# First loads, diagonals by two engines and the place of a table load in an attention and feed-forward kernel

## The chip, the cores and the metric

The kernel runs on one core of one Trainium2 chip. The metric is the device time of one execution in microseconds (us). Five engines work side by side: PE (matmuls; PEld is its weight loading), DVE (VectorE), ACT (ScalarE), POOL (GpSimd) and SP, which only issues DMAs here. Each engine runs its own instructions in a fixed order, so an instruction that waits holds up all that stand behind it on the same engine.

## The reference

Three parts follow each other. All is computed in float32.

1. A linear attention with a decaying state, 4 batches, 8 heads, 768 tokens, 48 elements per head:

```
cur   = (u * k_t) outer v_t
y_t   = r_t @ (state + cur)
state = w * state + k_t outer v_t
```

2. On the 3072 x 384 result a feed-forward layer with 2048 hidden units: `h = x @ w_in; g = h * tanh(softplus(h)); x = g @ w_out`.
3. A second one with other weights: `h = x @ w_in; g = h if h > 0 else exp(h) - 1; out = g @ w_out`.

## The kernel before, in words

The tokens are cut into 24 chunks of 128 (six to a batch), four chunks to a block of 512 columns. The attention of block 0 comes first, with the conversion of the first weights beside it; then the first layer runs block by block with the attention of the next block woven in; then the second layer.

**A chunk of attention.** Two loads bring it: KR (r and k with the head's elements on partitions, 448 KB) and KVR (k, v and r with tokens on partitions, 576 KB). The third chunk borrows the tiles HB1 and TB for its KR and KVR. DVE multiplies k and r of KR by powers of the decay (Tn, T) at line 405, and k of KVR by Trv. Then:

- *scores* (L541, 8 matmuls, traced as 16): k against r, 128 x 128 per head, into two PSUM banks.
- *diagonal* (L509, 4 matmuls): the sums of u*k*r for each token. DVE first makes the product k*r in the tile XO (L405); PE sums it over the partitions against um; ACT copies the 128 x 8 result to CD. XO is one tile, so the next chunk's product waits until PE has read it.
- *AB*: ACT (L531) puts CD on the diagonal of a 128 x 8 x 128 tile, one ACTIVATE per head, for chunks 0 to 3 (`ON_ACT = 4`); from chunk 4 on POOL does it in one AFFINE_SELECT (L533). DVE (L548, two COPY_PREDICATED) then puts the scores above the diagonal.
- *outputs* (L611, L615, L620): state against r, and v against AB, into bank 6 alone. ACT casts the result to XH, DVE takes the rest to XL (L639); bank 6 is free only then. The first chunk of a batch has no L611.
- *update* (L580): the new part of the state in bank 5; DVE adds it to the decayed state SS (L595), which ACT (L590) has decayed.

**Other names.** w_in and w_out are split into a high and a low part (wih, wil, woh, wol): a raw tile (HB0 for the first, RAW0 and RAW1 after it) is loaded, DVE makes the high bits (L714, L717, L719), ACT casts them (L420), DVE subtracts (L412). The first layer's first matmul is L755 (nine per tile of 512 columns), its second L807; ACT takes its result to HB, applies three functions in TB with table loads between (L780 to L783), and casts to GH; DVE subtracts to GL. The second layer is L755 again with L1007 to L1009.

**What sets the order.** All work is first recorded as operations with the tiles they read and write and a cost in us. A planner (`Graph.order`) then walks through time, and on each engine takes the ready operation of lowest rank. Its result is the fixed order of every engine. Its costs are assumptions; when an instruction really starts is decided on the chip by the semaphores. So a change in a cost or in what an operation reads and writes can move instructions anywhere behind it. Each use of a PSUM bank for scores or first-layer tiles takes the next one in a cycle (`next_bank`).

`tables` (L822 on) makes T, Tn and Trv; its function `turn` turns T on PE (L854) through bank 7, and ACT copies that to Trv. The list of first loads stands in L883 to L897: w, chunk 0, um (by ACT's queue), u, chunk 1, the first raw weights, chunk 2, two more raw weights.

## Time and profile before

| | |
|---|---|
| median of 3 runs | 941.93 us (940.3, 941.93, 955.51) |
| profiled execution | 945.41 us, its span 943.6 us |
| PE busy | 916.8 us (97%) |
| PEld, DVE, ACT, POOL busy | 777.2, 597.9, 505.7, 173.5 us |
| chain of waits | PE 85%, DVE 6%, ACT 4%, DMA 4% |
| DMA | 90.83 MB |

The span runs from the first to the last instruction of the profiled execution. Busy shares are means over stages with different limits; PE's 97% says that most of the span is bound by matmuls, and not what bounds the first 100 us.

### The profile page before, as it was taken

What the parts mean: (1) busy time and instruction counts of PE and PEld (TensorE: products, weight loads), DVE (VectorE), ACT (ScalarE), POOL (GpSimd) and SP (SyncE); (2) the same over time, 40 slices, a digit from 0 to 9 for tenths busy, and PEclk for the clock granted to TensorE, in tenths of its full rate; (3) what the DMA queues carried; (4) which work ended last, traced back from release to release, by engine and by line L of the source; (5) the groups of instructions that cost most, each with busy time, mean ns of one, the idle gap of its engine ahead of it and who ended that gap; (6) DMA issues with size and microseconds to landing.
All of it is one profiled execution on the core that took longest, in us unless ns stands there. A gap on an engine that the chain in (4) does not pass through costs nothing.

```text
span 943.6 us, 13890 instructions
## 1 busy us (share of the span) xinstructions
PE 916.8 (97%) x5770; PEld 777.2 (82%) x5770; DVE 597.9 (63%) x777; ACT 505.7 (54%) x650; POOL 173.5 (18%) x125
## 2 busy tenths in 40 slices
PE   7888999999999999999999999999999999999997
PEld 6766777888878888888888899888899889889896
DVE  6799996443644454344376898678766555654663
ACT  4596678776777876787799643321411312312211
POOL 0011044333522264330222423000000000000000
PEclk9997999999999999999999999999899999999999
DMA  8355442220211311121233434878600101000001
GB/s 275 136 173 168 162 146 68 73 93 26 78 45 46 105 64 45 57 68 46 59 130 101 131 130 163 285 259 276 229 1 22 47 1 34 34 1 34 1 0 38
DMA packets 33335, 90.83 MB, mean 96 GB/s; under 512 B 3312, under 2 KB 6512, under 8 KB 33264
## 3 DMA queue, kind: packets, MB, share of 16 engines
q1 hardware_dynamic: 32848, 89.86, 28.6%
q8 instruction: 47, 0.77, 0.3%
q14 instruction: 24, 0.20, 0.1%
q10 hardware_dynamic: 416, 0.00, 0.0%
HBM read 80.42 MB, written 9.44 MB: 95 GB/s over the span
## 4 chain that ended last, share of the span: by engine, by line
PE 85%; DVE 6%; ACT 4%; DMA 4%; issue 1%; SPq 0%; DVEq 0%; ACTq 0%
PE bank L755 39%; PE bank L807 19%; PE bank L1009 6%; PE bank L1008 6%; PE bank L1007 6%; PE bank L541 3%; PE bank L611 1%; DMA RAW<-w2i 1%; DVE KVR L735 1%; PE bank L615 1%; PE bank L620 1%; PE bank L580 1%; DVE GL L412 1%; PE bank L509 1%; DMA RAW<-w1o 1%
## 5 line engine op out<-in xcount | busy, mean ns | idle before, releaser
L755 PE MATMUL bank<-XH,wih 128*128 128x512 f32 x576 | 230.8, 401 | 5.5 <-ACT HB L420 4.7
L755 PE MATMUL bank<-XL,wih 128*128 128x512 f32 x576 | 228.3, 396 | 1.6 <-DVE XL L639 1.6
L755 PE MATMUL bank<-XH,wil 128*128 128x512 f32 x576 | 228.7, 397 | 0.0
L992 ACT ACTIVATE HB<-HB 128x512 f32<-128x512 f32 x96 | 60.6, 633 | 236.3 <-DVE HB L990 235.6
L412 DVE TENSOR_TENSOR GL<-HB,GH 128x512 fp32r<-128x512 f32 (+2 forms) x75 | 91.2, 1216 | 84.8 <-PE bank L807 83.4
L755 PEld LDWEIGHTS bank<-XH,wih 128*128 128x128 f32 x576 | 109.0, 189 | 29.8 <-ACT HB L420 5.6
L1007 PE MATMUL bank<-woh,GH 128*128 128x384 f32 x384 | 131.0, 341 | 2.0 <-DVE GH L422 1.7
L755 PEld LDWEIGHTS bank<-XH,wil 128*128 128x128 f32 x576 | 108.8, 189 | 26.8 <-DVE wil L412 0.3
L1008 PE MATMUL bank<-wol,GH 128*128 128x384 f32 x384 | 130.9, 341 | 0.0
L755 PEld LDWEIGHTS bank<-XL,wih 128*128 128x128 f32 x576 | 108.9, 189 | 24.5 <-DVE XL L639 1.9
L420 ACT CAST GH<-HB 128x512 fp32r<-128x512 f32 (+2 forms) x74 | 71.8, 970 | 67.8 <-DVE HB L993 38.1
L990 DVE TENSOR_SCALAR HB<-bank 128x512 f32<-128x512 f32 x96 | 65.9, 688 | 56.9 <-PE bank L755 56.7
L993 DVE SCALAR_TENSOR_TENSOR HB<-HB,bank 128x512 f32<-128x512 f32 x96 | 65.6, 684 | 38.1 <-ACT HB L992 37.6
L405 DVE TENSOR_TENSOR HB<-HB,TB 128x1536 f32<-128x1536 f32 (+1 forms) x36 | 62.9, 1746 | 42.0 <-ACT TB L783 42.0
L807 PE MATMUL bank<-GH,woh 128*128 128x512 f32 x288 | 85.9, 399 | 0.0
L420 ACT COPY HB<-bank 128x512 f32<-128x512 f32 x89 | 51.6, 585 | 62.0 <-PE bank L755 53.0
L807 PE MATMUL bank<-GH,wol 128*128 128x512 f32 x288 | 84.7, 395 | 0.0
L807 PE MATMUL bank<-GL,woh 128*128 128x512 f32 x288 | 84.6, 395 | 0.0
L1007 PEld LDWEIGHTS bank<-woh,GH 128*128 128x128 f32 x384 | 72.8, 190 | 6.2 <-DVE GH L422 2.0
L1008 PEld LDWEIGHTS bank<-wol,GH 128*128 128x128 f32 x384 | 72.9, 190 | 3.2
L1009 PE MATMUL bank<-woh,XL 128*128 128x384 f32 x216 | 73.5, 340 | 0.1
L807 PEld LDWEIGHTS bank<-GL,woh 128*128 128x128 f32 x288 | 54.1, 188 | 13.2
(126 smaller groups left out, 1298.0 us busy)
## 6 DMA issues: line engine op xcount, KB each, us to landing
KVR<-kvr SPq DMA_DIRECT2D x23, 576.0 KB, 5.0
RAW<-w1o SPq DMA_DIRECT2D x16, 768.0 KB, 4.4
RAW<-w2i SPq DMA_DIRECT2D x16, 768.0 KB, 4.3
RAW<-w2o SPq DMA_DIRECT2D x16, 768.0 KB, 4.3
RAW<-w1i SPq DMA_DIRECT2D x15, 768.0 KB, 4.3
KR<-rk SPq DMA_DIRECT2D x23, 448.0 KB, 4.1
x2d<-XO SPq DMA_DIRECT2D x18, 256.0 KB, 2.0
AB<-x2d SPq DMA_DIRECT2D x18, 256.0 KB, 2.9
```

Of the source, the lines that this page charges most:

```text
L405: ENG[e].tensor_tensor(out=o, in0=a, in1=b, op=ALU.mult)
L412: ENG[e].tensor_tensor(out=o, in0=a, in1=b, op=ALU.subtract)
L420: A.copy(out=o, in_=a)
L541: mm(bks[i][:, p * CH:(p + 1) * CH], X[half[i], g, 1, j], X[half[i], g, 0, j], start=True, stop=True)
L755: mm(hbk[:, :n], w[f][:, k, :], x[:, k, :n], start=(i == 0), stop=(i == len(seq) - 1))
L807: mm(acc[:, :n], w[f0 + j][:, d * P:(d + 1) * P], gg[:, j, :n], start=(q == 0 and i == 0), stop=(q == NG - 1 and i == len(seq) - 1))
L990: on(DVE, dve(n), [kb], [kg], lambda: V.tensor_scalar(out=g, in0=hbk[:, :n], scalar1=0.0, scalar2=None, op0=ALU.min))
L992: on(ACT, act(n), [kg], [kg], lambda: A.activation(out=g, in_=g, func=AF.Exp), AF.Exp)
L993: on(DVE, dve(n), [kg, kb], [kg], lambda: V.scalar_tensor_tensor(out=g, in0=g, scalar=-1.0, in1=hbk[:, :n], op0=ALU.add, op1=ALU.max))
L1007: mm(acc, gh[:, tt], woh[f], start=(f == 0), stop=False)
L1008: mm(acc, gh[:, tt], wol[f], start=False, stop=False)
L1009: mm(acc, gl[:, tt], woh[f], start=False, stop=(f == NF - 1))
```

## The change

- The load of KVR leaves r out for chunks 0 to 7 (`FROM_PE = 8`), which use the diagonal on PE and never read it: 384 KB in place of 576 KB, in two pieces of 1536 bytes per partition in place of one of 4608.
- u_sb (192 KB), first read in chunk 8, is loaded after the raw weights and not before chunk 1.
- For chunks 0 to 3 the diagonal sums go to the next bank of the cycle and not to bank 5, which they shared with the state's update.
- For the same chunks ACT puts four of the eight heads on the diagonal, and POOL the other four. The planner is told 1.23 and 0.7 us where it had 2.45, and 1.25 in place of 1.4 for POOL's later ones.
- `turn` uses bank 6 and not bank 7.
- A copy of one column by ACT into a CD tile stands ahead of its other work, so that its table load does too.

```diff
--- before.py
+++ after.py
@@ -461,7 +461,8 @@
         s["X"], s["t"] = X, t
         gr_keys.update(key(a, i) for a in (X, t) for i in range(3))
         dma(X.rearrange("p g m h t -> p (g m h t)"), rk[n], KP * 2 * CU * 4, [], [key(X, i) for i in range(2)])
-        dma(t, kvr[n], P * NHG * 3 * DU * 4, [], [key(t, i) for i in range(3)])
+        m = 2 if n < FROM_PE else 3
+        dma(t[:, :, 0:m], kvr[n][:, :, 0:m], P * NHG * m * DU * 4, [], [key(t, i) for i in range(m)])
 
     def early(n):
         return (DVE,) if n < EARLY else (DVE, POOL)
@@ -500,8 +501,11 @@
         kr = xo[0:KP, 0:CU].rearrange("p (g j t) -> p g j t", g=NHG, j=NP)
         kx = [key(xo), key(ident), key(rec)]
         mul(CU, kr, X[:, :, 1], X[:, :, 0][:, :, :, ::-1], [key(X, 0), key(X, 1)], kx, on=early(n))
-        dg = bank[UB][:, NHP * 2 * D:NHP * 2 * D + NHD]
-        kd = (id(bank[UB]), "diag")
+        if n < ON_ACT:
+            b = bank[next_bank(turn[0])]
+            dg, kd = b[:, 0:NHD], key(b)
+        else:
+            dg, kd = bank[UB][:, NHP * 2 * D:NHP * 2 * D + NHD], (id(bank[UB]), "diag")
 
         def prod():
             for p in range(NHP):
@@ -525,13 +529,14 @@
         bks = [bank[next_bank(turn[0])] for _ in range(2)]
         pairs = ab.rearrange("p (q i) t -> p i q t", i=2)
 
-        def diag(e):
-            if e == ACT:
-                for h in range(NHD):
-                    A.activation(out=ab[:, h], in_=flip, func=AF.Copy, scale=c[:, h:h + 1])
-                return
-            G.affine_select(out=ab, in_=c.rearrange("p (h o) -> p h o", o=1).to_broadcast([P, NHD, CH]),
-                            pattern=[[0, NHD], [1, CH]], compare_op=ALU.is_equal,
+        by_head = ab.rearrange("p (q i) t -> p q i t", i=2)
+
+        def diag_a():
+            for q in range(NHP):
+                A.activation(out=by_head[:, q, 0], in_=flip, func=AF.Copy, scale=c[:, 2 * q:2 * q + 1])
+
+        def diag_g(o, w):
+            G.affine_select(out=o, in_=w, pattern=[[0, o.shape[1]], [1, CH]], compare_op=ALU.is_equal,
                             fill=0.0, base=1 - CH, channel_multiplier=1)
 
         def prod():
@@ -540,7 +545,13 @@
                 for i in range(2):
                     mm(bks[i][:, p * CH:(p + 1) * CH], X[half[i], g, 1, j], X[half[i], g, 0, j], start=True, stop=True)
 
-        gr.add({ACT: 2.45} if n < ON_ACT else {POOL: 1.4}, [key(c), key(flip)], [key(ab, 0), key(ab, 1)], diag, port=(POOL,))
+        if n < ON_ACT:
+            on(ACT, 1.23, [key(c), key(flip)], [key(ab, 0)], diag_a)
+            on(POOL, 0.7, [key(c)], [key(ab, 1)], lambda: diag_g(by_head[:, :, 1], c.rearrange(
+                "p (q i) -> p q i", i=2)[:, :, 1:2].to_broadcast([P, NHP, CH])), port=(POOL,))
+        else:
+            on(POOL, 1.25, [key(c)], [key(ab, 0), key(ab, 1)], lambda: diag_g(ab, c.rearrange(
+                "p (h o) -> p h o", o=1).to_broadcast([P, NHD, CH])), port=(POOL,))
         yield 1.15, [key(X, 0), key(X, 1)], [key(b) for b in bks], prod
         gr.boost = BOOST
         for i in range(2):
@@ -847,7 +858,7 @@
             in1=rec[:, :, 0:16].rearrange("p q (o b) -> p q o b", o=1).to_broadcast(full), op=ALU.mult))
         on(DVE, 0.16, [kt, key(um)], [key(um)], lambda: V.tensor_tensor(
             out=um, in0=um, in1=T[:, :, 1:2].to_broadcast([KP, NHP, 2]), op=ALU.mult))
-        bk = bank[7]
+        bk = bank[YB]
 
         def turn():
             for p in range(NHP):
@@ -886,7 +897,6 @@
     for i in range(2):
         on(ACT, 0.45, [key(um)], [key(um)], lambda i=i: nc.scalar.dma_start(
             out=um[half[i], :, i], in_=uG[i:H:2].rearrange("q d -> d q")))
-    dma(u_sb.rearrange("p g e -> p (g e)"), uB, P * DM * 4, [], [key(u_sb)])
     load(1)
     raws[0] = fetch()
     load(2)
@@ -895,6 +905,9 @@
     done[0] = 2
     raws[2] = fetch()
     done[0] = 0
+    dma(u_sb.rearrange("p g e -> p (g e)"), uB, P * DM * 4, [], [key(u_sb)])
+    cd = CD.tiles[1]
+    on(ACT, 1.5, [key(nln2)], [key(cd)], lambda: A.copy(out=cd[:, 0:1], in_=nln2))
     on(POOL, 0.3, [], [key(ident)], setup_id)
     on(POOL, 0.5, [], [key(above)], setup_mask)
     on(POOL, 0.5, [], [key(flip)], setup_flip)
```

The planner's order moves in three places. First ACT, at its first work. Before (VT is a copy of v, from KVR of chunk 0 and chunk 1 in turn):

```order
L420 ACT_TABLE_LOAD
L420 COPY VT_139<-KVR_133 128x4x16 x2
L420 COPY Trv<-bank_80 128x4x48 x2
L420 COPY VT_140<-KVR_134 128x4x16 x2
L420 COPY CD_135<-bank_78 128x8
L531 ACTIVATE AB_137<-flip,CD_135 128x128 x8
L420 COPY CD_136<-bank_78 128x8
L531 ACTIVATE AB_138<-flip,CD_136 128x128 x8
```

Now:

```order
L910 ACT_TABLE_LOAD
L910 COPY CD_136<-nln_120 128x1
L420 COPY VT_139<-KVR_133 128x4x16 x2
L420 COPY VT_140<-KVR_134 128x4x16 x2
L420 COPY Trv<-bank_79 128x4x48 x2
L420 COPY CD_135<-bank_74 128x8
L536 ACTIVATE AB_137<-flip,CD_135 128x128 x4
L601 ACTIVATE SS_142<-SS_141,T 112x96 x4
```

The table load has gone to its own copy. The copies to Trv stand behind the VT copy of chunk 1 now, so behind the landing of chunk 1's KVR (KVR_134).

Then DVE, at the second chunk's product (XO<-KR_132). Before:

```order
L405 TENSOR_TENSOR KVR_134<-KVR_134,Trv 128x2x192
L714 TENSOR_SCALAR HB_125<-HB_125 128x768
L717 SCALAR_TENSOR_TENSOR HB_125<-HB_125 128x768
L405 TENSOR_TENSOR XO_143<-KR_132 112x512
L422 COPY SS_141<-bank_78 112x384
L405 TENSOR_TENSOR HB_126<-HB_126,Tn 112x2x256
L405 TENSOR_TENSOR HB_126<-HB_126,T 112x2x256
L548 COPY_PREDICATED AB_137<-above,bank_74 128x4x128
```

Now:

```order
L405 TENSOR_TENSOR KVR_134<-KVR_134,Trv 128x2x192
L725 TENSOR_SCALAR HB_125<-HB_125 128x768
L405 TENSOR_TENSOR HB_126<-HB_126,Tn 112x2x256
L405 TENSOR_TENSOR XO_143<-KR_132 112x512
L422 COPY SS_141<-bank_78 112x384
L405 TENSOR_TENSOR HB_126<-HB_126,T 112x2x256
L559 COPY_PREDICATED AB_137<-above,bank_80 128x4x128
L559 COPY_PREDICATED AB_137<-above,bank_75 128x4x128
```

The third chunk's first multiply (HB_126 with Tn), which needs that chunk's load, has moved ahead of the second chunk's product, and a weight operation (L717) has moved away behind it.

Last PE, at the end of block 0's attention. Before (the last scores of chunk 3, its diagonal, the outputs of chunk 2, the update, the first outputs of chunk 3):

```order
L541 MATMUL bank_74<-KR_131 128x128
L541 MATMUL bank_80<-KR_131 128x128
L509 MATMUL bank_78<-um,XO_143 128x2 x4
L611 MATMUL bank_79<-HB_126,SS_142 32x128 x4
L615 MATMUL bank_79<-AB_137,TB_127 32x128 x4
L611 MATMUL bank_79<-HB_126,SS_142 32x128 x4
L615 MATMUL bank_79<-AB_137,TB_127 32x128 x4
L611 MATMUL bank_79<-HB_126,SS_142 32x128 x4
L620 MATMUL bank_79<-AB_137,VT_139 32x128 x8
L580 MATMUL bank_78<-KVR_133 48x48 x8
L611 MATMUL bank_79<-KR_131,SS_141 32x128 x4
L615 MATMUL bank_79<-AB_138,KVR_133 32x128 x4
```

Now (the end of the outputs of chunk 2, all scores of chunk 3, its diagonal, the update):

```order
L622 MATMUL bank_79<-HB_126,SS_142 32x128 x4
L631 MATMUL bank_79<-AB_137,VT_139 32x128 x8
L546 MATMUL bank_77<-KR_131 128x128
L546 MATMUL bank_73<-KR_131 128x128
L546 MATMUL bank_77<-KR_131 128x128
L546 MATMUL bank_73<-KR_131 128x128
L546 MATMUL bank_77<-KR_131 128x128
L546 MATMUL bank_73<-KR_131 128x128
L546 MATMUL bank_77<-KR_131 128x128
L546 MATMUL bank_73<-KR_131 128x128
L513 MATMUL bank_76<-um,XO_143 128x2 x4
L591 MATMUL bank_78<-KVR_133 48x48 x8
```

The scores and the diagonal of chunk 3 stood ahead of the outputs of chunk 2 and stand behind them now, next to the outputs of chunk 3, which need that diagonal. In the same way the outputs of chunk 0 moved ahead of the diagonal and the scores of chunk 2.

## Rows read from the trace of the kernel before

**Rows 1.** How busy each engine is in four stretches: stretch, length, engines' busy us (instructions), PEclk, DMA share, GB/s.

```profile
9.10:36.20 27.10, 26.70 (x304) 23.57 (x304) 19.11 (x32) 15.65 (x54) 0.00 (x0) 1.00 0.60 212
...
40.90:57.00 16.10, 16.10 (x102) 13.48 (x103) 14.71 (x19) 12.31 (x17) 1.09 (x1) 1.00 0.42 130
57.00:90.70 33.70, 25.12 (x239) 19.98 (x239) 31.72 (x36) 27.26 (x33) 5.45 (x3) 0.91 0.59 190
90.70:900.00 809.30, 806.09 (x4869) 681.66 (x4870) 502.84 (x636) 438.91 (x523) 163.93 (x109) 0.99 0.27 90
```

**Rows 2.** The chain of waits, 0 to 60 us: start, us, engine, line, count.

```profile
6.95 1.28 ACT L420
...
9.12 2.07 PE bank L541 x14
...
24.10 0.58 PE bank L611 x8
...
26.39 0.85 PE bank L620 x16
...
28.05 2.01 PE bank L541 x16
30.06 1.80 PE bank L509 x8
...
47.24 0.79 PE bank L509 x8
48.02 1.09 PE bank L541 x16
```

**Rows 3.** The timeline, 13 to 45 us: start, us, engine, line, operation, [idle before, releaser].

```profile
34.28 1.35 DVE L548 COPY_PREDICATED AB<-above,bank 128x512 f32<-128x512 uint32 x2 [0.30 <-ACT AB L531]
...
35.44 0.89 ACT L420 CAST wih<-HB 128x768 fp32r<-128x768 f32 x1
...
36.19 0.65 PE L611 MATMUL bank<-KR,SS 112*32 112x128 f32 x8 [0.38 <-DVE XL L639]
36.23 1.17 ACT L590 ACTIVATE SS<-SS,T 112x96 f32<-112x96 f32 x4
36.36 0.96 DVE L412 TENSOR_TENSOR wil<-HB,wih 128x768 fp32r<-128x768 f32 x1 [0.23 <-ACT wih L420]
...
36.94 0.39 PE L611 MATMUL bank<-KR,SS 112*32 112x128 f32 x8
...
40.30 0.54 DVE L639 TENSOR_TENSOR XL<-bank,XH 128x384 fp32r<-128x384 f32 x1
```

**Rows 4.** The timeline of PE alone, 57 to 140 us.

```profile
61.22 0.43 PE L611 MATMUL bank<-KR,SS 112*32 112x128 f32 x8
...
62.35 0.62 PE L620 MATMUL bank<-AB,VT 128*32 128x128 f32 x16
...
90.73 0.80 PE L755 MATMUL bank<-XH,wih 128*128 128x512 f32 x1 [4.42 <-ACT HB L420]
```

**Rows 5.** The stretches again, for the first loads.

```profile
4.60:9.10 4.50, 2.81 (x10) 2.27 (x10) 2.63 (x6) 2.11 (x5) 0.00 (x0) 1.00 1.00 336
```

**Rows 6.** DMA issues of 4.1 to 4.6 us: the last number is us to landing.

```profile
HB<-rk SPq DMA_DIRECT2D x1, 448.0 KB, 10.4
```

**Rows 7.** The timeline, 0 to 45 us.

```profile
4.13 0.58 SPq L431 DMA_DIRECT2D HB<-rk  x1
...
9.37 0.69 DVE L405 TENSOR_TENSOR KR<-KR,Tn 112x512 f32<-112x512 f32 x1 [2.10 <-DMA KR<-rk]
...
14.11 2.45 ACT L531 ACTIVATE AB<-flip,CD 128x128 f32<-128x128 f32 x8
...
15.74 1.86 PE L509 MATMUL bank<-um,XO 112*128 112x2 f32 x8
```

**Rows 8.** GpSimd's diagonals (line 533): count, ns least/median/most.

```profile
L533 POOL TENSOR_SCALAR_AFFINE_SELECT AB<-CD x20: 1087/1094/2620, 52.4 to 419.6; 128x1024 f32<-128x1024 f32 x20
```

**Rows 9.** A stretch at half clock (columns as in rows 1).

```profile
88.01:94.84 6.83, 4.11 (x10) 3.24 (x11) 6.76 (x8) 2.42 (x4) 0.44 (x1) 0.50 0.32 117
```

## The prediction

> **What bounds the kernel now.** I read the stretches first [rows 1]. From 90.7 to 900 us PE is busy 806.1 of 809.3 us: there the time is matmul work, and the change touches none of its instructions. So its worth is what it shifts before 90.7, and that shift reaches the end if PE, which then has no slack, starts its unbroken stretch earlier or later. From 57.0 to 90.7 DVE is busy 31.7 of 33.7 us and PE waits (25.1 busy); PE's last long wait, 4.42 us, ends at 90.73 [rows 4] on a chain through DVE and ACT. From 40.9 to 57.0 PE is full (16.1 of 16.1), as it is from 9.1 to 36.2 (26.7 of 27.1). So until 57 a shift of PE is passed on, then one of DVE is.
>
> The chain of waits [rows 2] shows the first 36 us. ACT's table load ends at 8.23, PE's scores of chunk 0 go on at 9.12, and then nearly all is PE: scores 2.01 us, a diagonal 1.80, later outputs 3.14 (24.10 to 27.24). From 47 us on the same diagonal takes 0.79 and scores 1.09. [...] The place of the rise is seen in the timeline [rows 3]: L611 takes 0.65 us at 36.19 and 0.39 at 36.94. Warm outputs take 1.75 (61.22 to 62.97 [rows 4]). So the chain of block 0 runs at half clock for 27 us.
>
> **The change, part by part.** Chunk 0 is the first.
>
> *Loads.* Until the third chunk's k and r have landed, 3 x 192 KB less are ahead in the queue (r of chunks 0 and 1, and u): 0.59 MB. At 336 GB/s [rows 5] that is 1.75 us. The pieces fall to a third in size; if r's two thirds give only half of their 1.17 us back, 1.17 is left. No row here shows such a load, so the bounds are 0 and 1.75; I take 1.45, the middle of the two worked-out values. The third chunk's load landed at 4.13 + 10.4 = 14.53 [rows 6, 7]; now 13.1.
>
> *Table load and bank 6.* They free the scores of chunk 0 from Trv: all eight can start at 7.3 and not 9.12. That gain doesn't arrive whole. Chunk 0's diagonal needs its product, which stands on DVE behind chunk 1's first multiply, and that one waited until 9.37 for its DMA [rows 7]; with two of the three 192 KB gone, 8.3. Two multiplies of 0.69 more, and the diagonal starts near 9.7 in place of 11.19, and Trv, behind chunk 1's KVR now, still comes before the update needs it.
>
> *The second chunk's product.* On DVE it stands behind HB1's first multiply now, so behind the landing at 13.1. Two multiplies of 0.69 [rows 7]: 14.5. The second diagonal ran at 15.74 [rows 7], so PE is **1.24 us ahead** here. With no gain in the loads it would be 15.9, 0.2 behind.
>
> *Up to the outputs of chunk 1.* From 15.74 to 27.24 the same pieces ran as now run in another order (second diagonal and update, outputs of chunk 0, third diagonal, scores, outputs of chunk 1): 11.50 us. Now they end at 26.0. AB is no wait: ACT's half takes 1.23 (half of 2.45 [rows 7]), and POOL's at an estimate 0.55, half of the 1.09 of its full one [rows 8], beside ACT.
>
> *POOL and DVE.* The trace has a POOL diagonal of 2.62 beside the least, 1.09 [rows 8], so one can be held up or hold up. The four halves fall where DVE waits for a load, for scores or for ACT, so I cost them at nothing; the bound is one on the chain, 0.55. [...]
>
> *Block 0's end, the main point.* Outputs of chunk 2 need bank 6, free after cast and subtraction of chunk 1's: 27.05 (DVE's subtraction is 0.54 [rows 3], and I take the cast as no longer; the update of chunk 2 lies beside them). Before, the scores and diagonal of chunk 3 ran ahead of these outputs, which covered the way from the diagonal through ACT to AB. Now they follow them, and that way lies open: a copy by ACT (estimate 0.2), ACT's half 1.23, and on DVE both COPY_PREDICATED (1.35 [rows 3]) with a weight operation between them (an estimate of 0.55, as the like-sized 0.54). Its start depends on the clock:
>
> - *At half clock throughout:* 27.05 + 3.14 + 2.01 + 1.80 = 34.0 for the end of the diagonal; ACT's half ends at 35.45, AB at 37.35, where outputs of chunk 3 began at 36.19 before. ACT then decays the state (1.17) and casts wih (0.89): 37.5; from the subtraction that this cast releases (36.36) to the last XL (40.30) it was 3.94 [rows 3], so XL at 41.4: **1.1 us late**.
> - *Clock up from 27.05 on:* outputs 1.75, scores 1.09, diagonal 0.79, so 30.7; ACT's half ends at 32.1, decay and cast at 34.2, XL at 38.1: **2.2 us early**. AB, at 34.0, lets the outputs of chunk 3 run 2.2 earlier as well.
>
> Which one? Before, the clock rose at the end of a stretch of outputs and update alone (31.86 to 36.8, with a wait of 0.4), while stretches with scores or diagonals between them hadn't lifted it. The new order puts outputs, update and outputs together from 22.9 to 28.8 or later without one of those between. So I take the second. [...]
>
> *40.9 to 90.7.* DVE's order is the old one until near 75 us, so the shift passes. Behind it rows change places; the pieces that PE runs before its wait at 90.7 are the same. I take 0, with bounds of -0.6 and +0.4 (the subtraction that ends the wait has a wol operation ahead of it and two others behind it).
>
> The sum: -2.2 us. Against the profiled execution's 945.41 us that is 943.2; this execution stood 3.5 above the median of 941.93. On the median: **939.7 us**.
>
> **The rivals.**
>
> - *The clock stays down (slower).* The place is the diagonal of chunk 3; the price is the 1.1 us worked out above, and it decides if PE is still at half clock when the outputs of chunk 2 begin. For it: 27 us at half clock in the trace. Against it: the longer run of outputs. 943.0 us; if the first L755 matmuls run at half clock too, up to 1.7 more (half of 3.4 us), 944.7.
> - *The loads land no earlier.* Then the second diagonal starts at 15.95, 1.45 later than I have it: -2.2 + 1.45 = -0.75, 941.2 us. For it: DMA is the wait there [rows 7] and pieces get smaller. Against it: the bytes are gone.
> - *More comes back in 57 to 90.7.* PE stood idle for 4.42 us before 90.73 [rows 4], and from 88.01 to 94.84 it was at half clock, 4.11 us of it busy [rows 9]. If the other order of DVE and ACT keeps PE from falling idle so long, half of those 4.11 go as well: -4.3, 937.7 us. Nothing in the order promises it.
> - *The change does nothing that lasts:* DVE's 31.7 of 33.7 us eat the shift. 941.9 us.
>
> **How the numbers follow.** Forecast 0.50, clock down 0.25, no earlier landing 0.10, more in 57 to 90.7 0.10, nothing 0.05. The runs before lie from 940.3 to 955.5, so a median can be off by 2 us or so; the range of 935 to 946.5 holds the cases with that. About 2%, 18.8 us, is what a measurement of this kernel can tell from no change. To gain as much, nearly all of PE's waits before 90.7 would have to go; the slow side needs an execution such as the 955.5 to become the rule. So faster 0.02, within 2% 0.95, slower 0.03.
>
> **What would show it.** The loads: chunk 2's k and r landing near 13.1. The front: the second diagonal near 14.5, the outputs of chunk 1 ending near 26. The clock: matmul durations halving (L622 from 0.65 to 0.39) near 27 and not near 37. The end of block 0: AB of chunk 3 near 34, the unbroken first-layer matmuls from 38.7 in place of 40.9. PE's wait ending near 88.5 in place of 90.73. If the clock rises where it did, or PE's wait ends at 90.7 in spite of an earlier front, the forecast's step is wrong there.

## The result, and the profile after

The changed kernel takes 952.82 us (median of 20 runs, 948.24 to 959.93), the kernel before 942.91 us (20 runs) beside it: ratio 1.0108, 95% interval 1.0089 to 1.0128. It is slower by 1.1%: within the 2% that I gave most of the chance, but above the range of 935 to 946.5. The profiled execution took 956.99 us, with a span of 955.3.

The stretches of [rows 1], after:

```profile
9.10:36.20 27.10, 21.42 (x303) 18.52 (x299) 19.37 (x33) 12.99 (x46) 3.78 (x4) 1.00 0.61 188
...
40.90:57.00 16.10, 16.10 (x83) 13.20 (x82) 14.29 (x19) 10.96 (x16) 1.09 (x1) 0.91 0.33 108
57.00:90.70 33.70, 28.16 (x265) 22.14 (x265) 31.05 (x38) 27.47 (x33) 4.22 (x3) 0.90 0.54 168
90.70:900.00 809.30, 797.10 (x4808) 672.28 (x4808) 499.08 (x623) 438.93 (x524) 165.52 (x109) 0.99 0.27 91
```

PE is idle for 12.2 us from 90.7 on, where it was idle for 3.2. The waits of PE from 57 to 150 us (what waited, for whom: us in all, times, longest), after:

```profile
PE bank L546 <- ACT HB L420: 5.8, 2, 3.1
PE bank L766 <- ACT wih L420: 2.3, 1, 2.3
PE bank L766 <- DVE wil L412: 1.9, 1, 1.9
PE bank L622 <- DVE XL L650: 1.3, 1, 1.3
PE bank L818 <- DVE GL L412: 0.4, 1, 0.4
```

and before:

```profile
PE bank L755 <- ACT HB L420: 4.7, 2, 4.4
PE bank L541 <- ACT HB L420: 3.1, 2, 2.8
PE bank L611 <- DVE XL L639: 1.3, 1, 1.3
```

The waits of 2.81 us at 70.36 and of 4.42 at 90.73 [rows 4] are gone, and four others stand in their place, of 2.32, 1.87, 3.05 and 2.76 us, at 70.93, 73.94, 110.31 and 139.25. All waits together are 11.7 us, where they were 9.1. Behind the four the granted clock falls to 0.50 or stays there. The stretches at 0.50, after (length, PE busy, PEclk, DMA share, GB/s):

```profile
36.91:43.73 6.82, 5.46 (x39) 0.50 0.47 143
71.04:77.87 6.83, 4.96 (x13) 0.50 0.53 169
112.00:115.41 3.41, 3.41 (x10) 0.50 0.84 281
139.31:146.13 6.82, 6.82 (x26) 0.50 0.33 117
```

At 0.50 an L766 matmul of 128x512 starts every 0.43 us (74.53 to 76.67), at 1.00 every 0.23 (84.71 to 86.58). So nearly half of the busy time in these stretches is lost; I count half, an estimate. From 40.51 on, where the first layer's unbroken matmuls begin, this is (3.2 + 4.96 + 3.41 + 6.82) / 2 = 9.2 us; the 3.2 are the rest of the first stretch, which comes from block 0. Before, there was one stretch of 3.41 from 70.95 and the one of [rows 9], so at most (3.41 + 4.11) / 2 = 3.8. So by this estimate the clock costs 5.4 us more and the waits 2.6 more, 8.0 us together.

The order of the rows moves in more than the three places that are listed with the change. From 70 to about 180 us rows of PE, DVE, ACT, POOL and of the DMA queue have changed places too. PE's own scores of a chunk that is woven in, for instance, before:

```profile
70.36 1.57 PE L541 MATMUL bank<-KR 48*128 48x128 f32 x16 [2.81 <-ACT HB L420]
```

and after, behind a tile's 27 matmuls of L818 that they stood ahead of:

```profile
86.91 1.16 PE L546 MATMUL bank<-KR 48*128 48x128 f32 x16
```

The front, after (timeline of PE, and SP's issue of the third chunk's k and r):

```profile
4.29 0.74 SPq L431 DMA_DIRECT2D HB<-rk  x1
...
16.63 1.87 PE L513 MATMUL bank<-um,XO 112*128 112x2 f32 x8 [0.96 <-DVE XO L405]
...
25.77 0.66 PE L622 MATMUL bank<-KR,SS 112*32 112x128 f32 x8
...
26.62 0.42 PE L622 MATMUL bank<-KR,SS 112*32 112x128 f32 x8
26.87 0.61 PE L631 MATMUL bank<-AB,VT 128*32 128x128 f32 x16
...
35.11 0.41 PE L626 MATMUL bank<-AB,KVR 128*32 128x128 f32 x2 [1.76 <-DVE AB L559]
...
40.51 0.80 PE L766 MATMUL bank<-XL,wih 128*128 128x512 f32 x1 [0.79 <-DVE XL L650]
```

That load lands 11.0 us behind its issue (10.4 in [rows 6]), at 15.29:

```profile
HB<-rk SPq DMA_DIRECT2D x1, 448.0 KB, 11.0
```

The clock rises near 26.6, PE then waits for AB, the clock falls again (0.50 from 36.91 to 43.73), and the unbroken stretch begins where it began: at 40.51 (40.90). The rise is read from durations: up to 26.6 the granted clock reads 1.00, as it does up to 36.8 before. Scores take 2.08 us at 22.91 and 1.16 at 30.36; at 139.25, where the granted clock reads 0.50, 14 of the 16 rows take 2.04. So up to the first rise "half clock" and the rise itself, here and in the runs below, stand for such durations; that the clock is what makes them long was my estimate, and no row shows it.

**Three parts of a span** carry the rest of this text: up to the first matmul that reads XL (block 0, 40.90 before); from there to the first matmul of 128x384 (first layer, to 542.41 before); the second layer. In this pair of executions the difference of 11.7 is -0.4, +7.9 and +4.2. The last column is the ratio with its interval; all parts are from one profiled execution. Beside v1 to v18 the kernel before took 943.9 to 945.6 us, and the ratios go by that. The medians count all executions; the ratios leave out those that took over 1.5% more than the fastest of the same kernel (among the versions one each of v1, v10 and v13 and three of v15), and v15's profile is of one of these.

| version | block 0 | first layer | second | median us | ratio to before |
|---|---|---|---|---|---|
| before | 40.90 | 501.51 | 401.19 | 942.91 | |
| after | 40.51 | 509.43 | 405.36 | 952.82 | 1.0108 [1.0089, 1.0128] |
| v1 edits, order of before | 38.62 | 503.32 | 400.76 | 946.05 | 1.0004 [0.9973, 1.0034] |
| v2 same, new rows in block 0 | 40.56 | 505.26 | 405.08 | 951.53 | 1.0059 [1.0030, 1.0089] |
| v3 edits, new rows behind block 0 | 35.88 | 507.37 | 402.25 | 951.66 | 1.0086 [1.0054, 1.0118] |
| v4 no edits, new rows behind block 0 | 36.05 | 506.45 | 402.90 | 953.76 | 1.0092 [1.0057, 1.0128] |
| v5 as v1, k and v in one piece | 34.12 | 502.72 | 402.86 | 943.69 | 0.9996 [0.9960, 1.0032] |
| v6 as v1, new rows 57 to 90 us | 37.22 | 504.13 | 404.15 | 946.84 | 1.0016 [0.9985, 1.0047] |
| v7 as v1, new rows from 90 us | 40.75 | 508.96 | 401.39 | 952.80 | 1.0088 [1.0059, 1.0116] |
| v8 as v1, dense start | 40.19 | 501.63 | 400.68 | 947.43 | 1.0005 [0.9974, 1.0036] |
| v9 as v7, two rows back | 40.57 | 506.78 | 402.75 | 954.61 | 1.0094 [1.0056, 1.0131] |
| v12 as v7, wait filled | 40.02 | 509.99 | 408.29 | 952.40 | 1.0066 [1.0037, 1.0094] |
| v13 as v7, two other rows back | 38.39 | 508.20 | 408.31 | 949.41 | 1.0036 [1.0006, 1.0066] |
| v14 rows of v9 and v13 | 36.24 | 509.46 | 403.60 | 951.65 | 1.0055 [1.0019, 1.0092] |
| v17 as v14, two more | 38.34 | 507.12 | 401.14 | 951.46 | 1.0057 [1.0027, 1.0087] |
| v18 the change, bank count put back | 40.87 | 503.60 | 401.93 | 949.00 | 1.0047 [1.0012, 1.0081] |
| v16 as v2, wait filled | 42.23 | 505.62 | 400.55 | 950.07 | 1.0066 [1.0038, 1.0093] |
| v10 as v5, dense start filled | 33.61 | 501.21 | 399.18 | 942.11 | 0.9961 [0.9934, 0.9988] |
| v11 as v5, two waits filled | 34.82 | 502.49 | 400.29 | 942.91 | 0.9978 [0.9954, 1.0002] |
| v15 both | 38.76 | 500.12 | 407.42 | 941.90 | 0.9953 [0.9920, 0.9986] |

The rows of the second layer stand in one order in all of these, and it took 399.2 to 408.3 us. So its part of a single pair of profiles says nothing of the change.

### The profile page after: what moved, and what is told of

It is laid out like the page before. It is cut to its first block, busy times and chain, and to the rows that moved or that the text cites. A ratio compares the mean times of both kernels' runs of the same rounds, so it can differ in the third digit from the quotient of the medians.

```text
span 955.3 us, 13890 instructions
## 1 busy us (share of the span) xinstructions
PE 918.9 (96%) x5770; PEld 776.7 (81%) x5770; DVE 600.6 (63%) x777; ACT 501.9 (53%) x636; POOL 177.6 (19%) x128
## 4 chain that ended last, share of the span: by engine, by line
PE 74%; DVE 10%; DMA 9%; issue 2%; ACT 2%; POOL 1%; SPq 0%; DVEq 0%; POOLq 0%; ACTq 0%
PE bank L766 34%; PE bank L818 19%; PE bank L1022 5%; PE bank L1020 5%; PE bank L1021 5%; DMA RAW<-w1i 2%; PE bank L546 2%; DMA RAW<-w2i 2%; DVE KVR L746 2%; DMA RAW<-w1o 1%; PE bank L622 1%; DMA HB<-rk 1%; DVE GL L412 1%; DVE RAW L728 1%; POOL wol L412 1%
## 5 line engine op out<-in xcount | busy, mean ns | idle before, releaser
L766 PE MATMUL bank<-XH,wih 128*128 128x512 f32 x576 | 231.5, 402 | 2.9 <-ACT wih L420 2.3
L766 PE MATMUL bank<-XH,wil 128*128 128x512 f32 x576 | 229.7, 399 | 1.9 <-DVE wil L412 1.9
L766 PE MATMUL bank<-XL,wih 128*128 128x512 f32 x576 | 229.4, 398 | 0.8 <-DVE XL L650 0.8
L766 PEld LDWEIGHTS bank<-XH,wil 128*128 128x128 f32 x576 | 109.4, 190 | 29.4 <-DVE wil L412 2.6
L766 PEld LDWEIGHTS bank<-XH,wih 128*128 128x128 f32 x576 | 109.3, 190 | 27.2 <-ACT wih L420 2.6
L766 PEld LDWEIGHTS bank<-XL,wih 128*128 128x128 f32 x576 | 109.4, 190 | 23.9 <-DVE XL L650 1.3
L405 DVE TENSOR_TENSOR HB<-HB,TB 128x1536 f32<-128x1536 f32 (+1 forms) x36 | 66.6, 1849 | 43.0 <-ACT TB L794 42.8
L818 PE MATMUL bank<-GH,woh 128*128 128x512 f32 x288 | 86.7, 403 | 0.0
L818 PE MATMUL bank<-GL,woh 128*128 128x512 f32 x288 | 85.4, 398 | 0.4 <-DVE GL L412 0.4
L818 PE MATMUL bank<-GH,wol 128*128 128x512 f32 x288 | 85.3, 398 | 0.0
L818 PEld LDWEIGHTS bank<-GL,woh 128*128 128x128 f32 x288 | 54.3, 189 | 14.2 <-DVE GL L412 1.1
```

What stands on the lines that cost most here:

```text
L405: ENG[e].tensor_tensor(out=o, in0=a, in1=b, op=ALU.mult)
L766: mm(hbk[:, :n], w[f][:, k, :], x[:, k, :n], start=(i == 0), stop=(i == len(seq) - 1))
L818: mm(acc[:, :n], w[f0 + j][:, d * P:(d + 1) * P], gg[:, j, :n], start=(q == 0 and i == 0), stop=(q == NG - 1 and i == len(seq) - 1))
```

## The experiments

**Edits or order?** Two lines replace the planner's order by one that is written out; all else is as edited.

```diff
-        for op in gr.order():
-            op.fn(op.eng)
+        for i, e in HELD:      # a list of operations and engines
+            gr.ops[i].fn(e)
```

v1, v2 and v3 have the change's edits, v4 none. (v1, v2 and all later written-out lists have the bank count of before behind block 0, `hcnt[0] -= ON_ACT`.) Lists: v1 that of before, v2 new in block 0 alone, v3 and v4 new behind it.

> All edits of the change, but every instruction in the order in which the kernel before runs it. Theory O (the planner's new order between 57 and 146 us is what costs the time: the outputs are PE's extra waits of 5.8 us for ACT HB and 4.2 for wih and wil): 941 to 943.5 us, ratio 0.998 to 1.001. Rival F (the new order of block 0, which lets the clock fall again at 36.9): 941 to 943.5 as well. Rival E (the edits themselves, loads in two pieces that slow the first transfers, or work moved between engines): 950 to 953, ratio 1.008 to 1.011.

> All edits of the change, its order in block 0, the order of before behind it. Theory O: 942 to 944.5 us (at most the 1.0 us by which the first layer's update ended later, 57.95 against 56.92), ratio 0.999 to 1.002. Rival F: 949 to 953, the whole loss. Rival E: 950 to 953.

> All edits of the change, the order of before in block 0, the change's order behind it. Theory O: 949 to 952.5 us, ratio 1.007 to 1.010, with PE waiting for HB near 110 and 139. Rival F: 941 to 944. Rival E: 950 to 953, and then the first version of this set, with the order of before, is as slow.

> None of the edits: the kernel before, its own block 0, and behind it the order of the change. Theory O: 949 to 953 us, ratio 1.007 to 1.011, for the order alone is enough. Rivals F and E: 942 to 944, as the kernel before.

v1 is as fast as before (1.0004): the edits by themselves cost and bring nothing that this measurement shows, and E falls. v4, without one edit, is 0.92% slower, and v3, with the edits, 0.86%: the order of rows behind block 0 is enough. With the order of before throughout (before, v1, v5, v8, v10, v11, v15) the first layer takes 500.1 to 503.3 us; with the new rows behind block 0 (after, v3, v4) 506.5 to 509.4. O holds for v3 and v4, but v2 doesn't fit it: the new rows of block 0 alone cost 0.59%, and its 951.5 us lie in F's range (PE waits 1.71 and 0.44 us for AB near 36, and the granted clock is 0.53 from 34 to 45). So each of the two parts of the new order is slow by itself. The two prices sum to about 1.4%, and the change lost 1.1%; the intervals are too wide to say whether they add up.

**Which rows behind block 0?** v6 and v7 split the list near its 300th operation, at about 90 us.

> All edits, order of before, except for 99 operations of the stretch from 57 to about 90 us, which stand in the change's order. Theory O1 (the loss comes from this stretch: PE's long wait of 4.4 us near 90 is exchanged for two near 66 and 69 for wih and wil and later ones for HB near 106 and 134, each with a stretch at half clock behind it): 950 to 953, ratio 1.006 to 1.009. Rival O2 (the loss comes from the order behind 90 us): 943.5 to 946.

> All edits, order of before up to about 90 us, the change's order from there on. Theory O1: 943.5 to 946.5, PE's wait of 4.4 us near 90 stays and those near 106 and 134 don't come. Rival O2: 950 to 953, with the waits for HB near 106 and 134.

O1, my choice, fell: nearly all of the loss comes with the rows from 90 us on. The waits that O1 named did come in v6 (2.32, 1.51 and 3.04 us), but the 2.8 near 70 and the 4.4 near 90 went for them. In v7 only one of the two waits that O2 named came, the one near 139. In v7, timelines of DVE, ACT and PE:

```profile
129.36 0.56 DVE L816 TENSOR_SCALAR RAW<-RAW 128x768 uint32<-128x768 uint32 x1 [2.29 <-DMA RAW<-w1o]
...
135.12 3.25 DVE L503 TENSOR_TENSOR GL<-HB,GH 128x1024 fp32r<-128x1024 f32 x1
...
138.46 1.07 ACT L511 COPY HB<-bank 128x512 f32<-128x512 f32 x2 [1.41 <-DVE GL L503]
...
139.09 2.07 PE L637 MATMUL bank<-KR 48*128 48x128 f32 x14 [3.00 <-ACT HB L511]
```

and in v1:

```profile
130.82 2.22 DVE L503 TENSOR_TENSOR GL<-HB,GH 128x1024 fp32r<-128x1024 f32 x1
...
133.12 0.59 ACT L511 COPY HB<-bank 128x512 f32<-128x512 f32 x1 [1.11 <-DVE GL L503]
...
133.85 1.16 PE L637 MATMUL bank<-KR 48*128 48x128 f32 x16
```

PE's scores need a bank that ACT empties into HB, and HB is free when DVE has subtracted for GL. That subtraction ends at 138.4 in v7 and at 133.0 in v1. So PE waits 3.00 us, and the granted clock reads 0.51 from 139.2 to 146. Four more runs, v9, v13, v14 and v17, ask whether single rows do it. On DVE and ACT, v9 (rows without a mark stay):

```diff
+L503 TENSOR_TENSOR GL_130<-HB_125,GH_128 128x1024
 L816 TENSOR_SCALAR RAW_146<-RAW_146 128x768
 L819 SCALAR_TENSOR_TENSOR RAW_146<-RAW_146 128x768
 L496 TENSOR_TENSOR HB_126<-HB_126,TB_127 128x1024
-L503 TENSOR_TENSOR GL_130<-HB_125,GH_128 128x1024
...
+L511 COPY HB_125<-bank_73 128x512
 L511 COPY VT_140<-KVR_133 128x4x16 x2
 L511 CAST GH_129<-HB_126 128x1024
-L511 COPY HB_125<-bank_73 128x512
```

> As the version with the change's order from about 90 us on (952.8 us), but two rows stand where the kernel before has them: on DVE the subtraction GL from HB and GH of 128x1024 ahead of the weights' pieces that wait for their transfer, on ACT the copy of a bank to HB ahead of VT and GH. Theory G (the loss of 7.3 us that the trace shows by 542 us is PE's wait of 3.0 us for that copy at 139.1 and the stretch at half clock behind it): the wait falls under 1 us, no half clock from 139 to 146, 945 to 948 us, ratio 1.000 to 1.003. Rival (the loss is spread over many rows of that order, or sits in the second layer): 950 to 953, ratio 1.006 to 1.009.

The loss stayed (954.6 us), as the rival has it. The scores no longer wait, but the next matmuls do, for the next copy to HB: v9's timeline:

```profile
139.61 0.80 PE L857 MATMUL bank<-XH,wih 128*128 128x512 f32 x1 [2.90 <-ACT HB L511]
```

v13 moves two rows of DVE near 120 us instead, v14 has both, v17 also the cast to XH and the subtraction to XL:

```diff
-L819 SCALAR_TENSOR_TENSOR RAW_146<-RAW_146 128x768
-L821 SCALAR_TENSOR_TENSOR RAW_146<-RAW_146 128x768
 L503 TENSOR_TENSOR GL_130<-HB_126,GH_129 128x1536
 L503 TENSOR_TENSOR wol_110<-RAW_145,woh_102 128x768
+L819 SCALAR_TENSOR_TENSOR RAW_146<-RAW_146 128x768
+L821 SCALAR_TENSOR_TENSOR RAW_146<-RAW_146 128x768
```

> The version with the change's order from about 90 us on (952.8 us), with two rows on DVE moved: the last two integer steps on the second RAW stand behind the subtractions to GL (128x1536) and wol, as before, not ahead of them. Theory R (these two rows hold up the subtraction that frees the first RAW by 1.9 us, so the load of w1o into it is issued at 123 and not 125 us, DVE waits 2.3 us less for it near 129, and HB comes earlier): DVE's wait for w1o under 0.8 us, PE's wait near 139 under 1.5 us, 946 to 949.5 us, ratio 1.001 to 1.005. Rival (the rows further down alone make HB late): PE waits 3 us again near 139, 951 to 954, ratio 1.006 to 1.010.

> The version before this one, and also the subtraction to GL of 128x1024 and the copy to HB where the kernel before has them. Theory R with both parts needed: PE's waits near 139 under 0.8 us in all, no stretch at half clock there, 944.5 to 947.5, ratio 0.999 to 1.003. Rival (the loss sits elsewhere, in the second layer or in the rows of POOL): 950 to 954.

> The version with both groups of rows put back (951.65 us), and also ACT's cast to XH ahead of the copy to HB near 124 us and DVE's subtraction to XL ahead of the multiply of HB, as before. Theory R2 (DVE's wait of 1.8 us for XH is the third piece of the delay): DVE's wait for XH goes, PE's wait near 138 falls under 1.5 us, the time from the first unbroken matmuls to the second layer falls from 509.5 to 503 to 506 us; 945 to 948.5 us, ratio 1.000 to 1.004. Rival (HB is held up by ACT's own table loads and sigmoid, which stand ahead of the copy in this order): wait 2 to 3 us as before, 508 to 510 us, 950 to 953.

The first link of R is right: DVE's wait for w1o falls from 2.29 to 0.7 us in v13. The second is wrong: DVE then waits 1.8 for XH, and PE 2.71 for HB. In v17 it is 2.12. From v13 (95 to 145 us):

```profile
DVE XL L741 <- ACT XH L511: 1.8, 1, 1.8
DVE RAW L816 <- DMA RAW<-w1o: 1.0, 2, 0.7
```

The first layer stays at 506.8 to 509.5 in v9, v13, v14 and v17: the delay isn't in the rows that were put back, each mended link lets the next one show. By the ratios v13, v14 and v17 (1.0036 to 1.0057) are lower than v7 (1.0088), with intervals that overlap; v13 lies in R's range, v14 and v17 (951.65 and 951.46 us) in those of their rivals. So that these rows bring nothing isn't shown either.

Two suspects are left untested, kinds of new rows that none of these runs puts back. PE's own rows are the first: a tile of nine L857 that ran at 110.8 us in v1 runs behind the following 27 matmuls in v7. The queue of loads is the second. In v1 the next chunk's KR is issued ahead of a weight load:

```profile
123.05 0.46 SPq L522 DMA_DIRECT2D KR<-rk  x1
...
127.49 8.91 SPq L522 DMA_DIRECT2D RAW<-w2i  x2
```

and in v7 behind it:

```profile
127.11 0.37 SPq L522 DMA_DIRECT2D RAW<-w2i  x1
127.53 0.46 SPq L522 DMA_DIRECT2D KR<-rk  x1
```

So POOL's multiplies of that chunk begin at 134.64 us in v7 and at 128.72 in v1, and stand beside DVE's work on HB later: in v9, where the subtraction has got out of their way, the multiply of HB takes 3.27 us (1.22 in v7). KR stands ahead of that weight load in before, v1, v6 and v18, whose first layers take 501.5 to 504.1 us, and behind it in after, v3, v4, v7, v9, v12, v13, v14 and v17, with 506.5 to 510.0. This is a coincidence of the two and no proof, since the other rows differ as well. Which set of rows would be enough was not found.

**What of it is the clock?** v12 puts work whose result nobody reads into PE's wait; bank 5 has 120 free columns:

```diff
+        def fill(n):
+            for _ in range(n):
+                mm(bank[UB][:, 392:512], flip, flip[:, 0:120], start=True, stop=True)
...
+        AHEAD_OF = {362: 20}
         for i, e in HELD:
+            if e == PE and i in AHEAD_OF:
+                fill(AHEAD_OF[i])
             gr.ops[i].fn(e)
```

> The version with the change's order from about 90 us on (952.8 us), with 20 matmuls of 128x120 whose result nobody reads put on PE ahead of the scores that wait 3.0 us near 139. The wait stays, PE is not idle in it. Theory H (half of the loss is the clock that falls behind the wait): full clock from 139 to 146, 949 to 950.5, ratio 1.004 to 1.006. Rival (the clock's fall costs nothing there, since PE waits again anyway): 952 to 954, ratio 1.008 to 1.010.

The fill was too long (4.55 us, the wait 3.0), and yet v12 is 0.2% nearer to before than v7 is. Behind it the granted clock reads 1.00 (v12, columns as in rows 1):

```profile
141.00:148.00 7.00, 7.00 (x42) 5.75 (x42) 6.86 (x8) 3.46 (x4) 3.21 (x2) 1.00 0.33 114
```

In v7, 139.2 to 146 reads 0.51. So by the rows the wait of 3.00 us in v7 is followed by a stretch that by an estimate costs some 3.4 us more (half of 6.8 busy), as H has it. As a gain in time it isn't shown: the medians are 952.4 and 952.8, v12's ratio lies between H's range and the rival's, and its first layer takes 509.99 us where v7's takes 508.96.

**Why did the planner sort anew?** `next_bank` hands out banks in a cycle. The four sums of diagonals take four more turns of it, so every later product lands in another bank. v18 is the change, sorted by the planner, with the count put back behind block 0:

```diff
         pack(n)
     gr.bias = B_MAIN
+    hcnt[0] -= ON_ACT
 
     def need(x, f):
```

> The change itself, sorted by its planner, with one line more: behind the four sums of diagonals the count that hands out the banks is set back by four, so that all later products use the banks that they use in the kernel before. Theory B (the count alone makes the planner sort the stretch from 57 us on anew, and badly): the time from the first unbroken matmuls to the second layer falls from 509.4 to 503 to 506 us; 946 to 950 us, ratio 1.002 to 1.006, what is left being the new order of block 0. Rival (any new order is as bad, or the planner's changed price for POOL's diagonal does it): 508 to 510 us in that stretch, 951 to 954, ratio 1.007 to 1.011.

B held: the first layer takes 503.60 and not 509.43, and the waits near 110 and 139 are gone. The ratio is 1.0047 in place of 1.0108, and the intervals don't meet. PE's waits of v18, 57 to 150 us, are those of before again:

```profile
PE bank L766 <- ACT HB L420: 4.7, 2, 4.3
PE bank L546 <- ACT HB L420: 3.1, 2, 2.8
PE bank L622 <- DVE XL L650: 1.3, 1, 1.3
```

The banks themselves are not it, since v4 has the banks of before and is slow. What v18 still loses (0.47%) is of the size of v2's loss, and block 0 stands in one order in both. That block 0 alone is the rest isn't shown: from 101 us on 16 rows of DVE, 17 of ACT and a few of PE and POOL stand elsewhere in v18 than before. v16 fills PE's wait for AB in block 0 (`fill(7)` ahead of the outputs of chunk 3):

> The version with the change's order in block 0 and that of before behind it (951.5 us), with 7 matmuls of 128x120 whose result nobody reads put on PE ahead of the outputs of chunk 3, which wait 2.1 us for AB. Theory F (the loss there is mostly the clock that falls behind this wait, from 34 to 45 us): full clock up to the first wide matmuls, 946 to 949, ratio 1.001 to 1.004. Rival (the wait itself and the later first layer are the loss): 950 to 952.5, ratio 1.005 to 1.008.

The rival's range came out: the ratio is 1.0066, as without the fill (1.0059). The clock stayed up to 41.9 us (granted: 1.00 from 28 to 41), and while PE waited 1.70 us for XL it fell all the same (0.61 from 41 to 45). F's price is not settled: the clock behind AB isn't the whole of it.

**The loads.** v5 stores k, v and r of a chunk one behind the other, in memory and in KVR:

```diff
-    KVR = ring(2, [P, NHG, 3, HG * D], F32, "KVR")
+    KV = ring(2, [P, 3, NHG, HG * D], F32, "KVR")
+    KVR = Ring([x.rearrange("p m g e -> p g m e") for x in KV.tiles])
-        dma(t[:, :, 0:m], kvr[n][:, :, 0:m], ...)
+        dma(t.rearrange("p g m e -> p m g e")[:, 0:m], kvr[n][:, 0:m], ...)
...
```

> As the first version (all edits, order of before), but k, v and r of a chunk lie in the order k, v, r in memory and in KVR, so that the load of k and v alone is one piece of 3072 bytes for each partition in place of two of 1536. Theory (small pieces eat what the missing 0.59 MB should give): the third chunk's k and r land 1 to 1.5 us earlier than in the first version (14.9 us), near 13.5, and SP issues such a load in 0.42 us, not 0.55 to 0.65. Rival (the transfers are slow there for another reason, for instance DMA being shared with the weights): 14.5 to 15. In the time at most 1.5 us by either, so 943 to 946.5, which this measurement can't tell from the first version.

The third chunk's load, v1 and then v5 (issued at 4.30 and 3.65):

```profile
HB<-rk SPq DMA_DIRECT2D x1, 448.0 KB, 10.6
```

```profile
HB<-rk SPq DMA_DIRECT2D x1, 448.0 KB, 8.5
```

In this pair the same bytes land at 14.9 with two pieces of 1536 bytes per partition and at 12.15 with one of 3072: 2.75 us, 0.65 of it because the load is issued earlier. SP took 0.55 to 0.65 us to issue a load in two pieces, and 0.42 and 0.43 for the first two in one piece (0.60 for the third). The pair is an extreme one. Over all profiles this load lands at 12.15 to 13.84 with one piece (v5, v10, v11, v15), at 14.09 to 16.4 with two (fourteen profiles), and at 14.53 and 13.93 with the loads of before (before, v4). So one piece lands earlier, by some 1.6 us between the middles of the two groups; whether it is the size of the pieces or their number, no run separates. The time doesn't show it (0.9996), as expected.

**The clock of block 0.** v8 fills PE's first 7 us with five matmuls of 128x256; they write over the bank that DVE has cleared for the state's update, so the state isn't the reference's.

> The first version (all edits, order of before) with five matmuls of 128 columns of weights and 256 columns of ones ahead of and behind the first one, written to a bank that nothing reads, in the 7 us in which PE waits for the first loads. Theory C (PE's clock rises once PE has been busy with wide matmuls, and small ones keep it up): matmuls of block 0 at full clock from 8 to 15 us on, block 0 ends 6 to 10 us earlier, 936 to 941, ratio 0.990 to 0.996. Rival (small matmuls don't hold the clock, or the rise comes when it comes): full clock not before 20 us, 943 to 947, ratio 0.998 to 1.002.

The rival was right. The clock was up at 7.33 (scores 1.16 us and not 2.07), fell at 12.30, behind PE's wait of 1.82 us, and the small matmuls stayed at half clock to 36 us (mean granted clock of the span 0.979, in v1 0.990):

```profile
7.33 1.16 PE L637 MATMUL bank<-KR 48*128 48x128 f32 x16 [0.27 <-DVE KR L496]
10.31 1.05 PE L604 MATMUL bank<-um,XO 112*128 112x2 f32 x8 [1.82 <-DVE XO L496]
...
14.75 1.87 PE L604 MATMUL bank<-um,XO 112*128 112x2 f32 x8 [1.31 <-DVE XO L496]
...
21.53 1.87 PE L604 MATMUL bank<-um,XO 112*128 112x2 f32 x8
```

v10 has v5's loads, a dense start of ten such matmuls (into bank 4), and `fill(6)` and `fill(10)` ahead of the first two diagonals. v11 has v5's loads, and `fill(16)` and `fill(28)` in the waits near 64 and 84 us. v15 has both, with fills of 3, 6, 11 and 18 and a dense start of five.

> All edits, order of before, k and v as one piece (943.7 us), with wide matmuls of ones in PE's wait for the first loads and small ones ahead of the first two diagonals, whose results nobody reads. Theory C (PE's clock rises behind wide matmuls and stays up as long as PE doesn't wait): full clock in nearly all of block 0, 937 to 941, ratio 0.990 to 0.996. Rival (the small matmuls of block 0 let it fall again, as behind the dense start alone): half clock from 12 us on for 10 to 25 us, 943 to 947, ratio 0.997 to 1.002.

> All edits, order of before, k and v as one piece (943.7 us), with 16 and 28 matmuls of 128x120 whose result nobody reads in PE's two waits of 2.8 and 4.4 us for HB (near 64 and 84 us). Theory H: the two stretches at half clock behind these waits (1.7 and 3.4 us lost) go, 939.5 to 941.5, ratio 0.994 to 0.998. Rival (the chain through DVE and ACT is the bound there, so a faster PE only waits again): 943 to 945, ratio 0.998 to 1.001.

> All edits, order of before, k and v as one piece, a dense start and filled waits as in the two versions tried (942.1 and 942.9 us), with the fills cut to the size of the waits (in those they ran 1.6 to 2.3 us over them). Theory: the two gains add up and the overshoot goes, 935 to 939, ratio 0.989 to 0.994. Rival (the gain is given back at later waits for transfers and by the second layer): 940 to 943, ratio 0.994 to 0.998.

In v10 the clock stays up through block 0, though the fills run over and hold up the first diagonals:

```profile
8.96 1.16 PE L638 MATMUL bank<-KR 48*128 48x128 f32 x16
...
19.77 1.05 PE L605 MATMUL bank<-um,XO 112*128 112x2 f32 x8
...
33.61 0.50 PE L858 MATMUL bank<-XL,wih 128*128 128x512 f32 x1 [1.33 <-DVE XL L742]
```

By the ratios v10 and v15 beat both kernels, by 0.4% and 0.5% of the time before; by the medians over all twelve executions v15's gain is 0.2% (941.90 against 943.94). In v10 the clock does what C says; 942.1 us lies between C's range and the rival's. v11 (0.9978, up to 1.0002) isn't told from before: its two stretches at half clock are gone, but its fills ran longer than the waits, and its first layer takes 502.49 us where v5's takes 502.72. v15 came out in its rival's range and isn't told from v10, so that the gains add up isn't shown. Its dense start of five did not lift the clock in its profile, where it rose at 24.47 us only; the scores of chunk 0 ran at half clock:

```profile
8.37 2.08 PE L638 MATMUL bank<-KR 48*128 48x128 f32 x16
```

What v15's profile does show is a first layer of 500.12 us.

## Why the prediction was wrong

- **Loads** (14.53 to 13.1): wrong. 15.29 in this profile, and 14.09 or later in all fourteen with these loads: no gain. The rival that the loads land no earlier had this right. I bounded the gain by 0 and 1.75 and left out that two small pieces could cost as much as the missing bytes give; the landings with one piece (12.15 to 13.84) say that they do. With pieces of 1536 and of 3072 bytes the load behind them lands some 1.6 us apart.
- **Second diagonal** (14.5) and **outputs of chunk 1** (26.0): 16.63 and 27.48. The diagonal is 0.89 us behind where I had 1.24 ahead, since the multiplies ahead of it waited for the load that landed at 15.29.
- **Clock near 27**: right in place (26.6), by luck. I read it off the order of the matmuls. With the very same block 0 as before, the clock rose near 21.8 us in v4; with one order and the same edits near 29.6 in v1 and 22.2 in v3. In the eleven profiles that have the order of before in block 0, the loads of before or of the change, and no added matmuls there, it rose between 21.8 and 36.8 us, and the profile that I forecast from is the latest of them. From v4:

```profile
20.23 1.08 PE L705 MATMUL bank<-AB,KVR 128*32 128x128 f32 x16
21.09 0.99 PE L710 MATMUL bank<-AB,VT 128*32 128x128 f32 x16
22.00 1.05 PE L599 MATMUL bank<-um,XO 112*128 112x2 f32 x8
```

  The two traces of one block 0 lie 15 us apart (21.8 and 36.8); what sets the moment among such small matmuls stays open. Much of the spread of block 0 in the table, 33.6 to 42.2 us, goes with it: 36.05 with the rise at 21.8 (v4), 35.88 at 22.2 (v3), 38.62 at 29.6 (v1), 40.90 at 36.8 (before).
- **AB near 34, first-layer matmuls from 38.7**: 36.2 and 40.51. I did price AB's open way, but took PE to be at full clock behind it. PE waited 1.76 and 0.68 for AB, and the granted clock fell to 0.50 at 36.91. That the gain of clock would be lost again behind the next wait was in no rival. v2 prices the new order of block 0 at 0.59%, where I had it as a gain.
- **"40.9 to 90.7 ... I take 0", and nothing at all behind 90.7**: here the forecast failed. I read PE's 806.1 busy of 809.3 us [rows 1] as a stretch that the change doesn't touch, since it touches no instruction there, and held the pieces that PE runs ahead of 90.7 for the same. The bank count made the planner sort all engines anew from 70 to about 180 us, PE's scores at 70.36 among them, and PE's being full rested on that order. Price in the profile: 7.9 us of the first layer, by the estimate from the rows 5.4 of clock and 2.6 of waits; by the ratios 0.9% (v3, v4 and v7). v18 gives 5.8 us of the first layer back by one count.
- **Rivals**: none held the loss. The slowest of them ended at 944.7 us, and it put its loss into block 0. No row ahead of the prediction shows the 3.4 us that it halves; in the trace before, the stretch at 0.50 from 70.95 is 3.41 long. "The change does nothing that lasts" is what v1 shows of the edits.

## What to carry to other kernels

An edit that takes one more turn of a shared count (banks, buffers) can re-sort all that a planner places behind it: compare the order of every engine to its end, and hold the old order when an edit is to be judged by itself. A stretch in which PE is full is not safe from such a change: its fullness rests on the order of all engines and of the loads (from 90.7 to 900 us PE is idle for 12.2 us here, where it was idle for 3.2). And one profile shows only one of the places at which the clock can rise (here between 21.8 and 36.8 us): a forecast that gains from an earlier rise should first see how far it moves between executions of one order.

## What the runs showed of the hardware

- PE's waits near 64 and 84 us in v5 (2.8 and 4.4 us) went with stretches at half clock (64.47 to 67.89 and 81.54 to 88.37), as before (granted clock 0.50 from 70.95 to 74.36 and from 88.01 to 94.84). Filled with matmuls that nobody reads they did not: v11, PEclk 1.00 at both places.

```profile
61.40:68.00 6.60, 6.47 (x57) 5.67 (x55) 5.61 (x8) 4.91 (x9) 0.00 (x0) 1.00 0.59 156
80.20:95.00 14.80, 14.73 (x92) 13.12 (x93) 14.66 (x18) 5.31 (x7) 1.97 (x1) 1.00 0.35 131
```

- Small matmuls kept PE busy for 22.2 of 23.9 us at half clock in v8 (12.30 to 36.20: diagonals in 1.87 us, 1.05 ahead of it) without lifting it before; the longest wait in between was 1.31 us.
- Subtractions on DVE took longer beside POOL's multiplies: that of 128x1024 1.22 us alone (v9, 132.12) and 3.25 in v7 beside two multiplies of POOL, and it ended 1.09 us behind the second of them; that to wol (128x768) in the profile after 0.95 at 126.97, with POOL idle, and 1.74 at 138.45, beside two of POOL's.
- The second layer, with one order in all runs, took from 399.2 to 408.3 us. Where it was long, DVE waited longer for weights that are loaded there: 28.1 us in all in v13 (408.3) and 18.1 in the kernel before (401.2). A single profile of the whole kernel can't be read to better than that.
